# Folding w3 into w_out and setting attention phases between FFN half units

## The chip, the cores and the metric

One core of one Trainium2 chip. The metric is device time in microseconds (us) of the slowest core, here the only one, as the median of several executions.

## The reference

```python
# q, k, v: (8, 8, 576, 64) float32, heads 0-3 "local", heads 4-7 "strided"
scores = q @ k.T / 8
rel = pos[:, None] - pos[None, :]
mask_local   = (rel >= 0) & (rel < 32)
mask_strided = (rel >= 0) & (pos[None, :] % 32 == pos[:, None] % 32)
attn = softmax(where(mask, scores, -1e9)) @ v
x = attn as (4608 tokens, 512)
h = ((x @ w1) * (x @ w2)) @ w3        # w1, w2: 512x1024, w3: 1024x1024
out = h @ w_out                       # w_out: 1024x512
```

There is nothing between `@ w3` and `@ w_out`, so the two can be one matrix of 1024x512.

## The kernel before

Attention is computed for one pair of heads at a time. Local heads use tiles of 96 queries against 128 keys. Strided heads are first sorted by residue class, 7 classes of 18 tokens to a tile of 126. The FFN works on 384 tokens at a time (12 chunks). Five of its first halves are issued among the attention; the rest runs afterwards. All cuts are marked with `...`.

```python
def emit_ffn_ab(tch, pool):                      # first half: (x w1) * (x w2)
    for jc in range(8):
        for ci in range(4): nc.tensor.matmul(aps, w1h[:, ci, js], xT[ci][:, tok], ...)
        nc.scalar.copy(out=asb, in_=aps)
        for ci in range(4): nc.tensor.matmul(bps, w2h[:, ci, js], xT[ci][:, tok], ...)
        nc.vector.tensor_mul(abt[:, jc, :], bps, asb)

def emit_ffn_rest(tch):                          # second half
    for jc in range(8):                          # h = ab @ w3
        for ci in range(8):
            nc.tensor.matmul(hps, w3h[:, ci, js], abt[:, ci, :], ...)            # L142
        nc.scalar.copy(out=hts[:, jc, :], in_=hps)
    for ts in range(3):                          # out = h @ w_out
        for ci in range(8):
            nc.tensor.matmul(ops, hts[:, ci, bass.ds(ts*P, P)], woh[:, ci, :], ...)
        ...

def emit_att(b):
    for hp in range(4):
        ...
        # strided pairs: evict the transposed q or k and sort it by class
        nc.scalar.copy(                                                          # L175
            out=_ap(tT, 0, [[pit, P], [4, 4], [1, 4], [18, 32]]),   # writes 36 bytes apart
            in_=tp0.rearrange("p c (j1 j0) -> p c j1 j0", j0=32))   # reads in order
        ...
        for hj in range(2):                      # one head after the other
            ...                                  # scores, exp, mask, values, normalise, transpose
        # strided pairs: back into token order
        nc.vector.tensor_copy(                                                   # L264
            out=_ap(xT[cc], S * b, [[NTOK, P], [1, 32], [32, NB]]),
            in_=_ap(xPc, 0, [[S, P], [NB, 32], [1, NB]]))

for b in range(8):
    if b == 1: emit_weights()
    emit_att(b)
    if 2 <= b < 7: emit_ffn_ab(b - 2, psAB_)
for c in range(12):                              # after all attention
    if c not in abts: emit_ffn_ab(c, _pf)
    emit_ffn_rest(c)
```

The softmax here doesn't subtract the row's maximum and nothing guards it: scores larger than these inputs give would overflow.

## Time and profile before

| | before |
|---|---|
| time, median | 579.07 us (573.91 to 583.76) |
| profiled span | 574.6 us |
| TensorE busy, mean granted clock | 499.6 us, 0.906 |
| attention stage, 0 to 302 us | TensorE busy 233.8 us, clock 0.84 |
| FFN stage, 302 to 575 us | TensorE busy 265.9 us, clock 0.98 |

The page of the kernel before: the busy times of the engines, then the TensorE, clock and DMA rows of the 40 slices (each digit is tenths of a slice of 14.4 us), then the chain of waits by line.

```profile
PE 499.6 (87%) x3201; PEld 301.2 (52%) x3201; DVE 189.4 (33%) x657; ACT 289.2 (50%) x477; POOL 150.5 (26%) x243
...
PE   4868845888888898987868999999999999999997
...
PEclk9999955599999899886555999999999999999999
DMA  7998695658868687576620111111101010101001
...
PE hps L142 22%; PE ops L148 10%; PE aps L126 10%; ACT tT L175 9%; PE bps L131 9%; PE sps L231 5%; PE tps L249 4%; PE xps L241 4%; ACT pte L232 2%; DMA vts<-in_v_dram 1%; DVE xqs L244 1%; ACT w3h L115 1%; DVE xT_113 L264 1%; ACT asb L129 1%; DVE ptm L238 1%
```

The clock numbers need one caution: where a page has no record of the granted clock yet, it counts full speed. The record begins at 53.8 us in this trace. Before that, 96-column transposes (L249) start 80 ns apart, as they do in stretches recorded at clock 0.5 (80 ns at 262 to 313 us), and not 43 ns as at clock 1. So TensorE ran at half clock there too.

The busy share of 87% is an average over two stages with different limits. A table by stage shows it; the columns are the stretch, its length, busy time of TensorE, its weight loads, VectorE, ScalarE and GpSimd, then the clock, the DMA share and GB/s.

```profile
0.00:302.00 302.00, 233.79 (x1677) 151.03 (x1677) 153.87 (x590) 194.87 (x287) 150.16 (x243) 0.84 0.73 117
302.00:575.00 273.00, 265.85 (x1527) 150.15 (x1525) 35.50 (x68) 94.33 (x190) 0.33 (x1) 0.98 0.10 36
```

The second stage is one stream of matmuls. Here is a piece of its timeline (start, duration, what, how many):

```profile
403.73 5.53 PE L142 MATMUL hps<-abt,w3h 128*128 128x384 f16 x33
409.10 5.34 PE L148 MATMUL ops<-woh,hts 128*128 128x512 f16 x24
```

A run of matmuls lasts (number - 1) starts plus the duration of the last, 0.38 us for 512 columns; so (5.34 - 0.38) / 23 = 215.7 ns from start to start. The same sum for 384 columns gives 162.4 ns.

In the first stage the engines wait for each other. One copy stands out, the sorting eviction at L175:

```profile
L175 ACT CAST tT<-tp_1289 x1: 2352/2352/2352, 118.5 to 118.5; 128x512 f16<-128x512 f32 x1
...
L264 DVE COPY xT_113<-xPc x8: 1408/1422/1428, 39.9 to 299.5; 128x576 f16<-128x576 f16 x8
...
L253 ACT COPY xT_111<-tps x16: 632/632/633, 17.4 to 279.6; 64x576 f16<-64x576 f16 x16
```

That is 2352 / 512 = 4.6 ns an element on ScalarE; the plain copy of 576 elements at L253 takes 0.632 us, 1.1 ns an element. In the view of who waited for whom, this copy has the longest line of TensorE (total us, times, longest):

```profile
PE sps L231 <- ACT tT L175: 21.5, 14, 2.4
```

### The profile page before, as it was taken

Reading aid. Unit: us, or ns where it says so; the run is one execution under the profiler, and the core shown is the slowest. Engines: PE = TensorE matmul, PEld = TensorE weight load, DVE = VectorE, ACT = ScalarE, POOL = GpSimd, SP = SyncE. Lnnn points to the kernel's source line nnn. Section 1 sums busy time; section 2 is a strip of 40 time slices with the busy share of each in tenths; the row PEclk is TensorE's granted clock in tenths of the full one; section 3 lists DMA queues with packets and bytes.
Section 4 is the critical chain, followed back from the end, with each engine's and each line's share of the span. In section 5 each row is a group of like instructions: output and inputs, shape, how many; then the busy total and the mean of one; then the engine's idle time right before and its main releaser. Section 6 shows DMA issues by size and latency. Waiting matters only on the chain.

```text
span 574.6 us, 8898 instructions
## 1 busy us (share of the span) xinstructions
PE 499.6 (87%) x3201; PEld 301.2 (52%) x3201; DVE 189.4 (33%) x657; ACT 289.2 (50%) x477; POOL 150.5 (26%) x243
## 2 busy tenths in 40 slices
PE   4868845888888898987868999999999999999997
PEld 2544423555555455555644555555565655555563
DVE  1454414547566575745543000003021111203030
ACT  2874777385766758484561333333333333333332
POOL 5652224355655538255450000000000000000000
PEclk9999955599999899886555999999999999999999
DMA  7998695658868687576620111111101010101001
GB/s 159 189 210 204 169 226 89 87 82 101 109 88 103 80 117 95 81 88 87 80 13 4 56 55 46 47 38 38 53 3 56 0 56 1 55 15 42 37 19 55
DMA packets 160443, 45.00 MB, mean 78 GB/s; under 512 B 152720, under 2 KB 152720, under 8 KB 160400
## 3 DMA queue, kind: packets, MB, share of 16 engines
q1 hardware_dynamic: 86160, 38.82, 24.8%
q0 software_dynamic: 74240, 5.63, 17.8%
q8 instruction: 25, 0.41, 0.3%
q14 instruction: 18, 0.15, 0.1%
HBM read 40.37 MB, written 9.44 MB: 87 GB/s over the span
## 4 chain that ended last, share of the span: by engine, by line
PE 72%; ACT 15%; DVE 5%; issue 3%; DMA 3%; SPq 1%; POOL 0%; DVEq 0%; ACTq 0%; POOLq 0%
PE hps L142 22%; PE ops L148 10%; PE aps L126 10%; ACT tT L175 9%; PE bps L131 9%; PE sps L231 5%; PE tps L249 4%; PE xps L241 4%; ACT pte L232 2%; DMA vts<-in_v_dram 1%; DVE xqs L244 1%; ACT w3h L115 1%; DVE xT_113 L264 1%; ACT asb L129 1%; DVE ptm L238 1%
## 5 line engine op out<-in xcount | busy, mean ns | idle before, releaser
L133 DVE TENSOR_TENSOR abt<-bps,asb 128x384 f16<-128x384 f32 x96 | 53.2, 555 | 233.9 <-PE bps L131 210.5
L142 PE MATMUL hps<-abt,w3h 128*128 128x384 f16 x768 | 129.4, 330 | 0.7 <-DVE xPc L260 0.7
L212 POOL DMA_DIRECT2D vts<-in_v_dram x160 | 99.8, 652 | 74.2 <-PE xps L241 34.6
L142 PEld LDWEIGHTS <-w3h 128*128 128x128 f16 x768 | 75.9, 99 | 52.7 <-issue 2.9
L144 ACT CAST hts<-hps 128x384 f16<-128x384 f32 x96 | 45.9, 478 | 91.1 <-PE hps L142 91.1
L129 ACT COPY asb<-aps 128x384 f32<-128x384 f32 x96 | 49.2, 514 | 44.4 <-DVE abt L133 37.8
L232 ACT ACTIVATE pte<-sps 128x288 f16<-128x288 f32 (+2 forms) x128 | 51.8, 440 | 30.0 <-PE sps L231 19.7
L231 PE MATMUL sps<-tT 64*128 64x96 f16 (+1 forms) x352 | 43.3, 248 | 25.6 <-ACT tT L175 21.5
L148 PE MATMUL ops<-woh,hts 128*128 128x512 f16 x288 | 64.1, 379 | 0.0
L131 PEld LDWEIGHTS <-w2h 128*128 128x128 f16 x384 | 36.9, 100 | 28.5 <-issue 6.7
L231 PEld LDWEIGHTS <-tT 64*128 64x128 f16 (+1 forms) x352 | 27.3, 134 | 45.4 <-ACT tT L175 28.0
L126 PEld LDWEIGHTS <-w1h 128*128 128x128 f16 x384 | 36.2, 101 | 26.5 <-issue 4.5
L241 PE MATMUL xps<-vts,ptm 128*96 128x65 f16 (+1 forms) x352 | 44.0, 243 | 2.4 <-DVE ptm L238 1.1
L249 PE MATMUL tps<-id128h,xqs 96*64 96x96 f16 (+1 forms) x352 | 35.7, 248 | 11.2 <-DVE xqs L244 10.5
L148 PEld LDWEIGHTS <-hts 128*128 128x128 f16 x288 | 28.2, 98 | 32.7
L151 ACT COPY osb<-ops 128x512 f32<-128x512 f32 x36 | 21.1, 585 | 44.5 <-PE ops L148 41.7
L241 PEld LDWEIGHTS <-ptm 128*96 128x96 f16 (+1 forms) x352 | 35.5, 160 | 13.8 <-DVE ptm L238 4.8
L249 PEld LDWEIGHTS <-xqs 96*64 96x64 f16 (+1 forms) x352 | 24.5, 130 | 30.5 <-DVE xqs L244 19.5
L126 PE MATMUL aps<-xT_111,w1h 128*128 128x384 f16 x96 | 32.7, 340 | 5.7 <-ACT asb L129 5.7
L204 POOL DMA_DIRECT2D vts<-in_v_dram x32 | 18.8, 586 | 65.9 <-PE xps L241 28.4
L126 PE MATMUL aps<-xT_113,w1h 128*128 128x384 f16 x96 | 32.7, 341 | 2.7 <-DVE xT_113 L264 2.7
L244 DVE TENSOR_TENSOR xqs<-xps,rcp 96x384 f16<-96x384 f32 (+1 forms) x64 | 34.1, 533 | 0.5
(430 smaller groups left out, 619.9 us busy)
## 6 DMA issues: line engine op xcount, KB each, us to landing
out_dram<-osb SPq DMA_DIRECT2D x36, 256.0 KB, 2.0
stg<-in_q_dram SPq DMA_DIRECT2D x64, 128.0 KB, 2.5
stg<-in_k_dram SPq DMA_DIRECT2D x64, 128.0 KB, 2.8
st<-in_moe_w_dram SPq DMA_DIRECT2D x4, 2048.0 KB, 7.7
vts<-in_v_dram POOLq DMA_DIRECT2D x32, 80.0 KB, 3.5
vts<-in_v_dram POOLq DMA_DIRECT2D x128, 15.8 KB, 2.6
st<-in_moe_w_out_dram SPq DMA_DIRECT2D x1, 2048.0 KB, 8.4
stg<-in_q_dram SPq DMA_DIRECT2D x64, 16.0 KB, 2.6
```

The costliest lines, as they stand in the source:

```text
L126: nc.tensor.matmul(aps, w1h[:, ci, js], xT[ci][:, tok], start=(ci == 0), stop=(ci == DM // P - 1))
L129: nc.scalar.copy(out=asb, in_=aps)
L131: nc.tensor.matmul(bps, w2h[:, ci, js], xT[ci][:, tok], start=(ci == 0), stop=(ci == DM // P - 1))
L133: nc.vector.tensor_mul(abt[:, jc, :], bps, asb)
L142: nc.tensor.matmul(hps, w3h[:, ci, js], abt[:, ci, :], start=(ci == 0), stop=(ci == DF // P - 1))
L148: nc.tensor.matmul(ops, hts[:, ci, bass.ds(ts * P, P)], woh[:, ci, :], start=(ci == 0), stop=(ci == DF // P - 1))
L175: nc.scalar.copy(out=_ap(tT, 0, [[pit, P], [4, 4], [1, 4], [18, 32]]), in_=tp0.rearrange("p c (j1 j0) -> p c j1 j0", j0=32))
L212: nc.gpsimd.dma_start(vts[0:18 * na, t, 0:D], _ap(v[b, h], 7 * t * D, [[D, na], [32 * D, NB], [1, D]]))
L231: nc.tensor.matmul(sps[0:krows, i, :], lhs, rhs, start=True, stop=True)
L232: nc.scalar.activation(out=pte[0:krows, 0:nt, :], in_=sps[0:krows, 0:nt, :], func=AF.Exp, bias=0.0, scale=scale)
L241: nc.tensor.matmul(xps[0:qt, t, :], ptm[0:krows, i, :], vts[0:krows, t, :], start=True, stop=True)
L249: nc.tensor.transpose(tps[bass.ds(crow, 64), t, 0:qt], xqs[0:qt, t, :], id128h[0:qt, 0:qt])
```

## The change

The intent has three parts. (1) w3 @ w_out is computed once on the chip, so that the h product disappears from every chunk. (2) Attention is cut so that strided tiles hold whole classes (72 tokens, 4 classes of 18) and the two heads of a pair share instructions; re-ordering copies now walk the output in order and put the stride on the PSUM read; q, k, v come in large pieces through the SP queue and GpSimd casts them. (3) Attention becomes a list of 7 short TensorE steps per pair (score group 0, transpose of the next q, score group 1, transpose of the previous output, value group 0, transpose of the next k, value group 1). The steps of batch t + 1 are placed one by one between the 24 half units of FFN tile t (512 tokens; four matmuls of 512 columns each), and each TensorE instruction is kept in program order. Below, a fold is the making of one of the eight row blocks of w3 @ w_out; the opening is the time before the first FFN tile; steps or tiles are bare when nothing is placed between them; an eviction is the copy of a TensorE result out of PSUM, where TensorE writes, into SBUF.

```diff
-    NT = 384
+    NT = 512
+    LQ, LT = 96, 6
+    SQ, ST = 72, 8
+    def pe(ins):
+        return tc.keep_in_program_order(ins)
 ...
+    def ph_T(s, which):                       # transpose of q or k, both heads of a pair
+        for c in range(n):
+            pe(nc.tensor.transpose(ps[:, c * w:(c + 1) * w], ...))
+        if s.local:
+            o, i = t[:, 0:S].rearrange("x (p c) -> x p c", c=n), ps[:, 0:S].rearrange("x (c p) -> x p c", p=w)
+        else:
+            o, i = t[:, 0:S], ps[:, 0:S]
+        if which == "q":
+            nc.scalar.copy(out=o, in_=i)
+        else:
+            nc.vector.tensor_copy(out=o, in_=i)
 ...
+    def ph_S(s, g):                           # scores, the two heads by turns
+        for i in range(m):
+            for h in range(2):
+                pe(nc.tensor.matmul(sps[:, h, i * w:(i + 1) * w], s.tT["k"][r, ks:ks + P], ...))
 ...
+    def ph_PV(s, g):                          # values; 128 weight columns, the tail is zeros
+                pe(nc.tensor.matmul(xps[:, h, i * 65:(i + 1) * 65], ptm[0:kr, c0:c0 + P], ...))
 ...
-        for jc in range(DF // P):
-            hps = psF[0].tile([P, NT], FP32, tag="hps")
-            for ci in range(DF // P):
-                nc.tensor.matmul(hps, w3h[:, ci, js], abt[:, ci, :], ...)
-            nc.scalar.copy(out=hts[:, jc, :], in_=hps)
+    def fold_halves(jc):                      # once: 8 transposes and 8 matmuls of 512 columns
+        def tr(): ...                         # w3 rows -> w3T, evicted by VectorE and ScalarE
+        def done(ps): nc.vector.tensor_copy(out=w34[:, jc, :], in_=ps)
+        return [tr] + acc_halves(lambda kc: w3T[kc // 4][:, kc % 4, js], lambda kc: woh[:, kc, :], done)
 ...
+    def host(units, upto):
+        n = len(units); p0 = pos[0]
+        for i, u in enumerate(units):
+            u()
+            tgt = p0 + ((upto - p0) * (i + 1)) // n
+            while pos[0] < tgt:
+                stream[pos[0]](); pos[0] += 1
 ...
+    load_wo(); load_w3(0); load_w3(1)         # the opening
+    for jc in range(4): ...                   # four folds, alone
+    load_local(0); load_w3(2); load_w3(3); load_strided(0); load_w12()
+    host(later, 14)                           # four folds between 14 attention steps
+    load_local(1)
+    att_only(batch_end[0])                    # the other steps of batch 0, bare
+    load_strided(1)
+    for tch in range(NTILE):                  # tiles 0 to 6 host batches 1 to 7; 7 and 8 are bare
+        units = ab_halves(tch) + o_halves(tch)
+        ...
```

## The prediction

> What bounds it now. The page's span is 574.6 us. A table by stage splits it at 302 us. After that only FFN runs: TensorE is busy 266 of 273 us at clock 0.98, so this stage is bound by matmul columns (24 matmuls of 512 columns ran in 5.34 us: 215.7 ns start to start). Before it, attention: TensorE 234 of 302 us at mean clock 0.84 (0.59 in 250-300 us). The chain of waits there is led by ScalarE's scattered q/k eviction (L175, 2.35 us each, 64 of them; 150 us of ScalarE), then small matmuls.
>
> What the change removes and adds, in TensorE columns:
> - Fold: the h product (768 matmuls x 384 columns) becomes a one-time 64 x 512 plus 64 transposes. 768 x 162.4 ns = 125 us goes, about 17 us comes. FFN then needs 864 matmuls of 512 columns = 186 us, all on the critical path.
> - Attention: a pair takes 42 (local) or 56 (strided) matmuls instead of 46 or 40, all small. In a warm stretch six transposes of 96 columns take 0.44 us (42 ns apart), 65-column ones 46 ns, 126-column ones 55 ns. I estimate 50 ns x 1568 = 78 us for all 32 pairs, about 10 us per batch.
> - Scattered writes disappear (the L175 evictions, the 1.42 us L264 copies): class-complete chunks make eviction writes contiguous and put the stride on the PSUM read. The Trainium skill ("SBUF — State Buffer", cachelines) says strides past a line pay, for both memories; this trace shows it for writes (4.6 ns per element at L175 against 1.1 at L253), and no line shows a strided PSUM read. I assume about 0.7 us for 576 elements.
> - V no longer goes through the GpSimd queue in small packets. GpSimd instead casts about 10,750 elements per partition per batch: estimated 11-20 us a batch.
>
> Per stage:
> 1. Start: about 12 us until w_out and the first w3 rows are in and cast, 16 us for four serial folds, about 20 us for four folds mixed with attention, about 20 us of latency-bound attention steps: about 68 us. Weight loads are not the limit (a 2 MB piece landed in 7.7 us).
> 2. Seven tiles, each hosting one batch: 96 x 216 ns = 20.7 us of FFN + 10 us of attention + 2-4 us of bubbles (the single transpose bank, a matmul behind GpSimd's zero fills, the tile's start behind the last xT eviction) = about 33.5, together 235 us. VectorE needs about 21 us and ScalarE about 15 us of each by this trace's durations, so TensorE bounds it; clock near 1.0.
> 3. Two bare tiles, 42 us, and a tail of 3.
>
> Sum about 348; I say 350 us, range 325 to 382. Faster by over 2%: 0.99; within 2%: 0.005; slower: 0.005.
>
> What would show it. Right: TensorE clock above 0.95 from about 70 us to the end; a steady 31-35 us per tile; no eviction of 576 elements above 1 us; the chain of waits over 75% TensorE. Wrong: strided PSUM evictions at 2 us or more (then ScalarE/VectorE head the chain, +40 us or more); GpSimd copies near 2 ns per element with TensorE waiting on zero fills; a clock of 0.5 in the opening lasting past 80 us.
>
> What would make it wrong. High side: the fixed TensorE order turns each late eviction into an idle TensorE; in-order VectorE queues hold weight casts ahead of attention; GpSimd and VectorE slow each other (the skill's "GPSIMD Engine Reference", key points, says they share SBUF interfaces; this trace has no such overlap). Low side: the 64-row score matmuls of two heads overlap in the array, and the opening loads run ahead.

## More of the kernel before

The times of one kernel in one set of rounds lie within 2% of each other, mostly within 1%.

## The result, and the profile after

| | before | after |
|---|---|---|
| time, median | 579.07 us (573.91 to 583.76) | 313.54 us (312.88 to 314.86) |
| profiled span | 574.6 us | 311.9 us |
| TensorE busy, mean clock | 499.6 us, 0.906 | 277.8 us, 0.965 |

The ratio is 0.543 (95% interval 0.539 to 0.547). Ratios here are the mean time of one kernel's runs over the mean of the other's in the same rounds, so not quite the ratio of the medians quoted. The direction and most of the size were foreseen, but 313.5 us lies under the stated range of 325 to 382.

The page of the changed kernel; a slice is now 7.8 us:

```profile
PE 277.8 (89%) x2561; PEld 144.2 (46%) x2561; DVE 188.9 (61%) x361; ACT 134.6 (43%) x221; POOL 100.3 (32%) x192
...
PE   0285757689999999999999999999999999999994
...
PEclk9999897569999999999999999999999999999999
DMA  6999999998769989999895868660002001102003
...
PE ops L317 26%; PE bps L303 20%; PE aps L294 20%; PE ps L201 5%; PE sps L224 5%; PE xps L250 4%; DMA st<-in_moe_w_dram 3%; PE ps L266 3%; ACT pte L229 2%; DVE w_115 L350 1%; ACT xT_112 L273 1%; DVE w3T_117 L346 1%; DVE xqs L258 1%; PE ps L344 1%; DVE t L212 1%
```

The clock record begins at 16.9 us here; the first fold's matmuls of 512 columns, before that, start 0.43 us apart, twice 0.216. Counted at 0.5, the mean clock would be about 0.94 instead of 0.965 (my estimate).

By stage (opening; seven tiles that host a batch each; two bare tiles and the tail), and then one hosted tile:

```profile
0.00:65.20 65.20, 36.80 (x351) 21.74 (x352) 33.43 (x63) 24.27 (x36) 21.34 (x48) 0.86 0.99 268
65.20:266.00 200.80, 199.23 (x2023) 103.71 (x2020) 141.17 (x279) 97.92 (x165) 78.98 (x144) 0.99 0.64 151
266.00:312.00 46.00, 41.77 (x196) 18.71 (x194) 14.27 (x21) 12.38 (x21) 0.00 (x0) 0.98 0.14 52
...
124.50:153.20 28.70, 28.44 (x293) 14.84 (x292) 19.64 (x40) 14.26 (x25) 13.20 (x23) 1.00 0.92 212
```

TensorE is busy 199.2 of 200.8 us in the middle. The view of its waits there (66 to 300 us) has one line:

```profile
PE aps L294 <- ACT xT_112 L273: 1.5, 6, 0.3
```

A tile repeats every 28.7 us. Inside it, steps and half units follow each other like this:

```profile
108.95 0.30 PE L224 MATMUL sps<-t 64*128 64x72 f16 x8
109.19 0.43 PE L266 MATMUL ps<-id_79,xqs 96*128 96x96 f16 x6
109.45 0.38 PE L294 MATMUL aps<-xT_109,w1h 128*128 128x512 f16 x1
...
110.32 0.41 PE L250 MATMUL xps<-v16S_103,ptm 72*128 72x65 f16 x8
110.56 0.38 PE L303 MATMUL bps<-xT_109,w2h 128*128 128x512 f16 x1
```

From the start of one line to the start of the next is what a step costs: 0.24 us for eight score matmuls, 0.26 for six transposes, 0.24 for eight value matmuls. On ScalarE, the re-ordering evictions that now read with a stride are no slower than plain ones (L210 is half the one and half the other). On VectorE they are: the 16 of L212 that read with a stride took 0.71 to 0.76 us, its 16 plain ones 0.40 to 0.46. Two lines of ScalarE, then VectorE's:

```profile
L273 ACT COPY xT_111<-ps x8: 632/632/640, 61.1 to 262.7; 128x576 f16<-128x576 f16 x8
...
L210 ACT COPY t<-ps x32: 626/640/646, 30.4 to 253.7; 128x576 f16<-128x576 f16 x32
...
L212 DVE COPY t<-ps x32: 397/584/758, 32.3 to 258.2; 128x576 f16<-128x576 f16 x32
```

### The profile page after: what moved, and what is told of

Read it like the earlier page. It is cut to its first block, busy times and chain, and to the rows that moved or that the text cites. A ratio compares the mean times of both kernels' runs of the same rounds, so it can differ in the third digit from the quotient of the medians.

```text
span 311.9 us, 6533 instructions
## 1 busy us (share of the span) xinstructions
PE 277.8 (89%) x2561; PEld 144.2 (46%) x2561; DVE 188.9 (61%) x361; ACT 134.6 (43%) x221; POOL 100.3 (32%) x192
## 4 chain that ended last, share of the span: by engine, by line
PE 83%; DVE 6%; ACT 5%; DMA 3%; issue 1%; SPq 0%; DVEq 0%; ACTq 0%
PE ops L317 26%; PE bps L303 20%; PE aps L294 20%; PE ps L201 5%; PE sps L224 5%; PE xps L250 4%; DMA st<-in_moe_w_dram 3%; PE ps L266 3%; ACT pte L229 2%; DVE w_115 L350 1%; ACT xT_112 L273 1%; DVE w3T_117 L346 1%; DVE xqs L258 1%; PE ps L344 1%; DVE t L212 1%
## 5 line engine op out<-in xcount | busy, mean ns | idle before, releaser
L297 ACT COPY asb<-aps 128x512 f32<-128x512 f32 x72 | 42.2, 586 | 68.8 <-PE aps L294 51.3
L229 ACT ACTIVATE pte<-sps 128x576 f16<-128x576 f32 (+1 forms) x64 | 41.6, 650 | 36.7 <-PE sps L224 36.1
L173 POOL CAST t<-st 72x1024 f16<-72x1024 f32 x32 | 33.0, 1059 | 25.0 <-DMA st<-in_q_dram 15.1
L154 POOL CAST t<-st 96x768 f16<-96x768 f32 x32 | 26.9, 867 | 29.2 <-DMA st<-in_q_dram 17.1
L201 PEld LDWEIGHTS <-t 72*128 72x128 f16 (+1 forms) x448 | 25.1, 101 | 17.0 <-issue 4.0
L201 PE MATMUL ps<-id_79,t 72*128 72x72 f16 (+1 forms) x448 | 28.5, 206 | 3.1 <-ACT w3T_118 L347 2.8
L250 PEld LDWEIGHTS <-ptm 72*128 72x128 f16 (+1 forms) x448 | 23.2, 101 | 17.2 <-issue 2.2
L236 DVE TENSOR_TENSOR ptm<-pte,maskS 72x576 f16<-72x576 f16 x32 | 19.3, 603 | 17.7 <-ACT pte L229 17.5
L294 PE MATMUL aps<-xT_112,w1h 128*128 128x512 f16 x72 | 27.5, 382 | 1.6 <-ACT xT_112 L273 1.5
L294 PE MATMUL aps<-xT_109,w1h 128*128 128x512 f16 x72 | 27.8, 386 | 0.0
L303 PE MATMUL bps<-xT_109,w2h 128*128 128x512 f16 x72 | 27.6, 384 | 0.0
L294 PE MATMUL aps<-xT_111,w1h 128*128 128x512 f16 x72 | 27.5, 382 | 0.0
L294 PE MATMUL aps<-xT_110,w1h 128*128 128x512 f16 x72 | 27.5, 382 | 0.0
L303 PE MATMUL bps<-xT_110,w2h 128*128 128x512 f16 x72 | 27.3, 379 | 0.0
L303 PE MATMUL bps<-xT_112,w2h 128*128 128x512 f16 x72 | 27.3, 379 | 0.0
L303 PE MATMUL bps<-xT_111,w2h 128*128 128x512 f16 x72 | 27.2, 378 | 0.0
```

The lines of the kernel that those rows point to most:

```text
L154: nc.gpsimd.tensor_copy(out=t[:, hp], in_=stv[:, 2 * hp:2 * hp + 2].rearrange("p h c d -> p c h d"))
L173: nc.gpsimd.tensor_copy(out=t[:, hp], in_=stv[:, 2 * hp:2 * hp + 2].rearrange("p h c d -> p c h d"))
L201: pe(nc.tensor.transpose(ps[:, c * w:(c + 1) * w], src[:, c].rearrange("p h d -> p (h d)"), id16[0:w, 0:w]))
L229: nc.scalar.activation(out=pte[0:kr], in_=sps[0:kr, :, 0:288], func=AF.Exp, bias=0.0, scale=scale)
L236: nc.vector.tensor_mul(ptm[0:kr, 0:576].rearrange("p (a x) -> p a x", x=w), pte[0:kr].rearrange("p h (a x) -> p (h a) x", x=w), _ap(maskS, ...
L250: pe(nc.tensor.matmul(xps[:, h, i * 65:(i + 1) * 65], ptm[0:kr, c0:c0 + P], vt[0:kr, 2 * (s.hp % 2) + h, g * m + i, :], start=True, stop=T ...
```

## The experiments

My theory after the result: the whole middle is matmul columns back to back; the h product's columns are simply gone; hosting takes away the waits; and my price for attention in a tile was too high, both per matmul and in waits. The rival readings are that one part (the pinned order, the overlap of two heads, the walk of the evictions) did nearly all of it. Five runs also ask what bounds the opening. Not tested alone are the loads in large pieces with GpSimd's casts, and that two heads share instructions; what these are worth is not shown.

### The fold, done alone in the kernel before

```diff
-        for jc in range(8):  ...  matmul(hps, w3h, abt) ; copy(hts, hps)
-                nc.tensor.matmul(ops, hts[:, ci, ...], woh[:, ci, :], ...)
+                nc.tensor.matmul(ops, abt[:, ci, ...], w34[:, ci, :], ...)
+        emit_fold()            # at the start of the FFN stage
```

> Kernel before, with w3 and w_out folded at the start of its FFN stage and the h product gone; attention untouched. Theory (the FFN stage is bound by matmul columns): 768 x 162.4 ns = 124.7 us goes, 64 x 215.7 ns + 64 transposes + waits = 17 to 22 us comes, so about 103 to 108 us less than before: 472 to 478 us; the attention stage stays at about 302 us. Rival (without the h product the evictions on ScalarE and VectorE bind the stage): less than 80 us saved, TensorE busy under 90% after 320 us.

Measured: 470.89 us against 577.01 in the same rounds (ratio 0.8135, interval 0.807 to 0.820), 106 us less. That is what the theory of matmul columns gave (103 to 108 us less), though 1 us under the range named for the total. TensorE is busy 145.1 of the 150 us from 320 us on, so the rival falls.

### The fold, taken out of the changed kernel

```diff
-        units = ab_halves(tch) + o_halves(tch)
+        units = ab_halves(tch) + h_halves(tch) + o_halves(tch)   # 16 half units more, evicted by ScalarE
-    (all fold_halves; w34)
+    (w3 and w_out kept as they are; fewer buffers for abt to make room)
```

> Changed kernel with the h product put back (64 more matmuls of 512 columns per tile, evicted by ScalarE), no fold, the attention steps spread over 40 half units per tile instead of 24. Theory (every tile is TensorE columns back to back): +9 x 64 x 215.7 ns = +124 us, less 5 to 17 us that the opening loses of folds, so 420 to 432 us; a tile grows from 28.7 to 42.5 us. Rival (the order of work and not the fold makes the gain): under 380 us.

Measured: 436.41 us (ratio 0.7529), 123 us more than the changed kernel, 4 us above the range I had named. The reason is instructive: the opening got only 1.5 us shorter (its first FFN matmul starts at 63.96 us instead of 65.44). So 124.2 - 1.5 = 122.7 us is the columns' full price, and the folds, about 17 us of TensorE work, cost almost nothing where they stand. (In three runs with the same order of opening, after_again, narrow_pv and scores_by_head, it started at 66.09, 64.12 and 64.87 us, so 1.5 us is not clear of scatter.) TensorE waits there for loads and casts instead: in this run's opening 36.1 us of its waiting ends with GpSimd's casts of q and k.

### TensorE instructions not kept in order

```diff
-        return tc.keep_in_program_order(ins)
+        return ins
```

> Changed kernel, TensorE instructions no longer kept in program order: the scheduler may move them. Theory (the fixed interleaving is what leaves no gap in the tiles): gaps come back, tiles grow from 28.7 us to 30 us or more, total 320 to 360 us. Rival (pinning is worth nothing, dependencies alone give the same order in effect): within 1% of the changed kernel, 311 to 317 us.

Measured: 312.92 us (ratio 0.5407, interval 0.537 to 0.545). The theory falls, the rival holds: pinning is worth nothing here. The scheduler moved some instructions (the first FFN matmul came at 49.62 us), but in the tiles it kept a stream almost without waits. Its tiles repeat every 28.31 us, 0.4 less than 28.71, but tile 0, begun early, took so long that both kernels reach tile 1 together (at 95.92 and 95.01 us). The placing of steps in the program does the work, not the pin.

### Attention steps not spread

```diff
             u()
-            tgt = ...
-            while pos[0] < tgt: ...
+        att_only(upto)         # after the units
```

> Changed kernel, same instructions, but each tile runs its 24 FFN half units first and then the attention steps of the next batch with nothing between. Theory (hosting hides the latency of the eviction chain): the unhosted opening ran 17 steps in 15.5 us, 0.91 us a step against 0.24 hosted, so 197 steps x 0.67 us = about +130 us: 410 to 460 us, with a lower clock in those stretches. Rival (the steps are cheap by themselves, pairs already overlap each other): under 350 us.

What ran is a little milder than that text says: a tile calls the placing twice, so it has two blocks of 12 units and 14 steps each. Measured: 402.42 us (ratio 0.6958), 89 us more, so hosting matters but under the 98 to 148 us that I had expected. Its middle by stage:

```profile
65.30:356.00 290.70, 245.68 (x2034) 130.99 (x2032) 149.34 (x279) 98.31 (x168) 79.37 (x144) 0.83 0.42 106
```

The 90 us have two halves. TensorE is idle 290.7 - 245.7 = 45 us instead of 1.6. And it is busy 245.7 us instead of 199.2 for the same instructions, because the granted clock is 0.83 instead of 0.99. The record shows the granted clock at 1 for 13.7 us and then at 0.5 for 6.8, over and over. No single wait in that stretch is longer than 1.43 us; the first line of its TensorE waits:

```profile
PE sps L224 <- DVE xqs L258: 23.1, 28, 1.4
```

### Attention steps in groups of four

```diff
+            if i + 1 < n:
+                tgt = p0 + 4 * ((tgt - p0) // 4)
```

> Changed kernel, attention steps set between FFN half units four at a time (S0 Tq S1 T2, then PV0 Tk PV1 S0) instead of one at a time; the same instructions. Unhosted (all 28 at once) costs +88 us or 12.6 us a tile. Theory (no bubbles because two half units, 1.7 us, lie between a step and the step that needs its eviction): T2 now follows Tq after 0.24 us and waits about 1.3 us for the bank, S0 follows PV0 after 0.5 us and waits about 1 us, so 2 us a pair, 6 to 10 us a tile: +40 to +70 us. Rival (any FFN work nearby is enough): under +10 us.

Measured: 354.26 us (ratio 0.6139), 41 us more, just inside what the theory gave for the total; the rival falls. The tiles repeat every 33.8 us, 5.1 more than in the changed kernel, a little under the 6 to 10 named. Its TensorE waits, over the whole run:

```profile
PE sps L224 <- DVE xqs L258: 19.7, 15, 2.7
PE ps L266 <- ACT t L210: 10.8, 18, 0.8
...
PE sps L224 <- DVE t L212: 9.6, 17, 1.1
```

The first two are the ones named beforehand: the scores that need a PSUM buffer back from the normalising product, and the transpose that needs the one transpose bank back from ScalarE. In the third, scores wait for the evicted k. The clock stayed at 1.00 (94 to 270 us), so here the loss is waiting alone. This shows why the bubbles that I had budgeted were missing: spread singly, a step has about two half units, 1.7 us, before its eviction is needed, and an eviction with its latency fits in.

### Walking the re-ordering copies the other way

```diff
-  o, i = t[:, 0:S].rearrange("x (p c) -> x p c", c=n), ps[:, 0:S].rearrange("x (c p) -> x p c", p=w)
+  o, i = t[:, 0:S].rearrange("x (p c) -> x c p", c=n), ps[:, 0:S].rearrange("x (c p) -> x c p", p=w)
   (and the same for the output of strided pairs)
```

> Changed kernel, the three re-ordering evictions (q and k of local pairs, the output of strided pairs) walk their elements the other way round: PSUM read straight, SBUF written with a stride of 12 or 16 bytes. Same values. Theory (the stride costs on the write and not on the read, and the fixed order then leaves TensorE idle): ScalarE's 32 such copies take 2.0 to 2.7 us instead of 0.64, VectorE's 16 take 1.2 to 1.5 instead of 0.6, and as the single transpose bank comes free only about 2.4 us later by schedule, tiles grow by 2 to 6 us: +15 to +45 us. Rival 1 (the slack between steps swallows it): copies as slow, but under +5 us. Rival 2 (the read side costs the same as the write side, or nothing does): the copies stay near 0.64 us.

Measured: 382.08 us (ratio 0.6626), 69 us more, over the top of my expectation. The lines of the three copies:

```profile
L210 ACT COPY t<-ps x32: 624/1357/2091, 30.9 to 319.2; 128x576 f16<-128x576 f16 x32
...
L212 DVE COPY t<-ps x32: 396/1232/2092, 33.5 to 323.7; 128x576 f16<-128x576 f16 x32
...
L273 ACT COPY xT<-ps x16: 2702/2710/2732, 69.2 to 331.7; 128x576 f16<-128x576 f16 x16
```

Minimum, median and maximum are in ns; half of the first two groups are plain copies and stayed fast. The turned ones went to 2.09 us on both engines (from 0.64 us on ScalarE and 0.75 on VectorE) and to 2.71 us. VectorE's was the surprise (I had said 1.2 to 1.5). The slack of 1.7 us no longer suffices; TensorE waits for these copies (below, 66 to 340 us), and the clock falls to 0.92 (95 to 203 us). Rival 1 and rival 2 both fall.

```profile
PE aps L294 <- ACT xT L273: 16.5, 8, 2.2
PE ps L266 <- ACT t L210: 16.4, 14, 1.8
```

### The same lesson in the kernel before

```diff
-    out=_ap(tT, 0, [[pit, P], [4, 4], [1, 4], [18, 32]]), in_=tp0.rearrange("p c (j1 j0) -> p c j1 j0", j0=32)
+    out=_ap(tT, 0, [[pit, P], [18, 32], [1, 16]]),        in_=_ap(tp0, 0, [[..., P], [1, 32], [32, 16]])
     (and L264 likewise)
```

> Kernel before, only the walk of two copies turned round: ScalarE's q/k eviction and VectorE's last re-ordering copy now write contiguous runs and read with a stride. Theory (the write side costs): 2.36 us falls to 0.55 to 0.7 us and 1.42 us to 0.3 to 0.8 us, 64 x 1.75 = 112 us less of ScalarE, of which the chain of waits (about 9% of the span in that copy) lets 35 to 80 us through: 500 to 545 us. Rival (four-dimensional walks cost, whichever side is strided): copies within 20% of what they were, and time within 2%.

Measured: 538.7 us (ratio 0.9339, interval 0.930 to 0.938), 38 us less for two turned walks with the same values. The copies:

```profile
L175 ACT CAST tT<-tp x32: 580/585/593, 22.0 to 260.0; 128x512 f16<-128x512 f32 x32
...
L264 DVE COPY xT<-xPc x16: 640/674/684, 36.4 to 269.0; 128x576 f16<-128x576 f16 x16
```

The walk at L264 has as many dimensions as before, so there the side of the stride alone made the difference, and the rival falls. This also shows a slip of mine, in the prediction and in the expectation: the copies are 32, not 64, so they cost 75 us of ScalarE and not 150. ScalarE's busy time fell from 289.2 to 236.5 us. The time landed in my range although the sum behind it was twice too large, which was luck.

### Value matmuls with narrow weights

```diff
-  matmul(xps[:, h, ...],    ptm[0:kr, c0:c0 + P], ...)
+  matmul(xps[0:w, h, ...],  ptm[0:kr, c0:c0 + w], ...)
```

> Changed kernel, value matmuls with 96 or 72 weight columns instead of 128 (the padding read no more). In the kernel before, such matmuls with 96 weight columns started 46 ns apart, and in the changed kernel with 128 weight columns 31 ns apart. Theory (my 50 ns per small matmul was too dear because it came from narrow weights; full weights load faster): the value steps grow from 0.18 and 0.24 us to about 0.28 and 0.33, 64 x 0.1 = +5 to +7 us in all. Rival (the width of the weights costs nothing, 65 streamed columns decide): under +1 us.

Measured: 316.83 us (ratio 0.5489, against 0.5426 for spread_fold, below, a run of the same rounds that is as fast as the changed kernel): about 3.5 us more. In the trace, local value steps went from 0.18 to 0.25 us (six matmuls, from 30 to about 45 ns apart), strided ones only from 0.24 to 0.28. The difference is real, and as the steps add up (32 x 0.07 + 32 x 0.035 = 3.4 us), but half of what I had expected: it explains 0.4 us of a tile, not the 3.3 that I was off in attention.

### Scores head by head

```diff
-        for i in range(m):
-            for h in range(2):
+        for h in range(2):
+            for i in range(m):
```

> Changed kernel, score matmuls of one head after those of the other, instead of alternating between the upper and lower 64 rows of the array. Now six start about 18 ns apart, but the step still takes 0.23 us to the next step's start. Theory (overlap of the two heads is nearly eaten up by a pause behind it): 6 x 41 or 8 x 33 ns = 0.25 us a step, +1 to +3 us in all. Rival (the overlap of two heads is what made attention cheap, as my low side had it): +8 us or more.

Measured: 315.01 us (ratio 0.5461), 1.5 us above the changed kernel, inside the theory and hardly above noise; by the traces, tiles repeat every 28.78 us instead of 28.71. A step takes 0.24 to 0.25 us instead of 0.23 to 0.24. But the edit did not do what the expectation took for granted: head by head, the matmuls still start close together (on average 17 and 21 ns apart, against 15 and 20 by turns), so this run shows no step without overlap. Another comparison settles it: in the changed kernel eight 72-column transposes take 0.259 us to the next start and eight 72-column score matmuls 0.236, and six of 96 columns 0.257 and 0.234. So overlap can be worth about 0.02 us a step, 0.2 us a tile; it is not what made attention cheap.

### The opening: five runs and a base

```diff
 spread_fold:   host(folds 4 and 5, 14 steps); host(folds 6 and 7, all other steps)
 local1_early:  load_w12 first half; load_local(1); load_w12 second half
 att_first:     load q, k, v of batch 0 first; 8 steps bare; folds 0-3 among the others; folds 4-7 in tile 0
 att_first2:    the same with 22 steps bare
 fold_late:     w1, w2 before w_out, w3; all steps of batch 0 bare; all folds in tile 0
```

> Changed kernel, the last four folds spread over all 31 opening attention steps instead of the first 14. The run without any fold had an opening of 64 us against 65, so folds seem to cost nothing there. Theory (the opening is bound by loads and the casts behind them): no change, within 2 us of the changed kernel. Rival (the 17 steps left bare are bound by latency, which FFN-like work would hide): opening 6 to 12 us shorter.

Measured: 312.32 us (ratio 0.5426): no change, first FFN matmul at 65.36 us. The bare steps were not what held it.

> The changed kernel once more, as the base for the runs on the same chip. Expected 311 to 315 us.

Measured: 315.16 us (ratio 0.5467, interval 0.545 to 0.549). The next two runs were made in the same rounds on the same chip.

> Changed kernel, only the order of loads in the opening changed: the first loads of batch 1 (which the opening's last steps need) go between the halves of w1 and w2 instead of behind them. The load queues were 99% busy over the opening's 65 us. Theory (the opening is bound by what is loaded before its last step): about 2 MB of w1 and w2 move behind the gate, at 268 GB/s about 7 us; 2 to 7 us faster than the changed kernel. Rival (the opening is bound by the latency of bare steps and folds, not by loads): within 1.5 us.

Measured: 312.09 us (ratio 0.5418, interval 0.540 to 0.544), 3 us or 0.9% faster than the changed kernel in the same rounds, with the first FFN matmul at 62.81 us against 66.09. The theory's low end, and the only version that is faster than the changed kernel clear of noise, by little.

> Changed kernel with a new opening: q, k, v of batch 0 are loaded first, its attention starts at once, four folds are hosted among its later steps, and the last four folds (with their w3 rows) are hosted in the first tile. Theory (the opening is bound by loads): tile 0 starts at about 45 to 50 us instead of 65, grows by 9 us of folds, and the total falls by 6 to 12 us to 301 to 307 us. Rival (bound by the latency of the steps, which a cold TensorE makes worse): tile 0 starts after 58 us and the total is not lower than 311 us.

Measured: 322.88 us (ratio 0.5599), 8 us slower. Tile 0 started earlier (60.43 us), but TensorE had stood 12.7 us at the first fold, whose w3 rows now came behind q, k and v:

```profile
31.00 1.04 PE L344 MATMUL ps<-id,t 128*128 128x128 f16 x8 [12.71 <-DVE t L130]
```

and the folds placed in tile 0 lengthened it. My theory, as I had turned it into an opening, lost.

> As att_first, but 22 opening steps run before the first fold, so that TensorE does not stand at a fold whose w3 rows are not there; four folds hosted on the last 11 opening steps, four in the first tile with their transposes one fold ahead. Theory (loads bound the opening, 17.5 MB by 65 us, and work can run under them): tile 0 starts at 46 to 52 us, total 303 to 309 us. Rival (latency of bare steps): tile 0 after 58 us, total 314 us or more.

Measured: 325.53 us (ratio 0.563), tile 0 at 62.15 us. TensorE stood 4.6 us at the fold and then 7.6 us for the casts of batch 1.

> Loads in the order q, k, v of batch 0, w1, w2 (batch 1 in between), then w_out and w3; opening attention bare, all eight folds in the first tile between its two halves. Theory (load-bound): tile 0 starts at 40 to 48 us, and the total is 302 to 309 us, as the 17 us of folds now lie under loads that still run until 65 us. Rival (latency of bare steps on a cold clock): tile 0 after 52 us and 314 us or more.

Measured: 336.55 us (ratio 0.5798). Tile 0 did start at 39.67 us, as I had expected, but then stood 9.4 us for batch 1's strided q and k, whose loads now came last, and the folds in the tile paused at each pass through the single transpose bank (1 to 1.8 us each); tile 1 started at 119.08 us, against 95.01 in the changed kernel. From tile 1 on, all these versions run 28.7 us a tile. An early start of tile 0 is worth nothing if the data that tile 0 must host comes later.

What bounds the opening stays partly open. Loads do in part (the earlier load gained 3 us; the queues are 99% busy), folds and bare steps by themselves do not, and three attempts to use the time better by another order failed.

## Why the prediction was wrong

Added by stage, prediction against profile: opening 68 against 65.2 us; seven hosted tiles 235 (33.5 each) against 200.8 (28.7 each); two bare tiles with the tail 45 against 46. **The step that failed is number 2, "20.7 us of FFN + 10 us of attention + 2-4 us of bubbles"**: 34 of the 36 us by which the sum missed are there. The mechanism was right (TensorE bounds the tile), two of its terms were mis-sized:

- *"I estimate 50 ns x 1568"*, 10 us a batch. Measured: the 28 steps of a batch (12 transposing steps of 0.26, 8 score steps of 0.235, 4 value steps of 0.18 and 4 of 0.24) make 6.7 us, which is 34 ns for each of 196 matmuls. I had averaged spacings of the old kernel's 96-, 65- and 126-column matmuls over a kernel whose matmuls have 65, 72 or 96. Against 50 ns each, the values made 1.1 us less, the scores 0.9, the 72-column transposes 0.8 and the 96-column ones 0.3. The section "Back-to-back issue gap" of the Trainium skill's page "TensorE: Matmul & The Clock Gate" has the form that would have served: columns / 2.4 + 2.5 ns, so 32.5, 42.5 and 29.6 ns for 72, 96 and 65 columns. (The section gives it for matmuls by themselves and has other figures for streams; those do not fit here, see the end.) The traces show medians of 32, 42 and 30 (transposes, transposes, values), and 215.7 against 215.8 for 512 columns. An estimate of 6.8 us a batch from it (24 x 42.5 + ... for each kind) would have been right. Neither the full-width weights (0.4 us a tile) nor the overlap of two heads (at most about 0.2) is the main cause.
- *"2-4 us of bubbles"*. Measured: 0.26 us of waiting a tile, and about 1 us at the joints between steps and units (28.7 - 20.7 - 6.7 = 1.3 in all). Most of that stands in one place: a score step starts 0.311 us after the last 512-column matmul before it, other steps 0.216 us after; 8 x 0.095 = 0.8 us. What makes this pause is not shown. I had seen the single transpose bank as a risk without setting the 1.7 us of FFN work between two uses of it against an eviction of 0.64 to 0.75 us. The run in groups of four brought 5.1 us a tile back, mostly at the waits I had named, so the spreading is the cause.

Point by point, the rest:

- The FFN stage as pure columns, 125 us out: right; 106 us net when done alone, 123 us when undone.
- About 17 us for the folds: near as work (with them TensorE is busy 36.8 us in the opening, without them 16.7, part of it at half clock), wrong as time. Taking them out shortened the opening by 1.5 us. The opening's total of 68 was near, but as a sum of serial pieces it was right for a wrong reason: loads and casts run beside them.
- "Weight loads are not the limit": wrong for the opening. The DMA share was 0.99 over its 65.2 us, and moving one load forward gained 3 us; one piece's landing time of 7.7 us did not show how full the queues would be.
- "Scattered writes disappear", about 0.7 us for a strided PSUM read: right; 0.63 to 0.64 us on ScalarE, 0.71 to 0.76 on VectorE. The count of 64 copies and 150 us of ScalarE was wrong (32, 75 us).
- VectorE about 21 us and ScalarE about 15 us a tile: 19.6 and 14.3. GpSimd 11 to 20 us of casts a batch: 13.2 with its fills. TensorE never waited for it in the tiles.
- Clock over 0.95 from the opening on: 0.99. The chain of waits over 75% TensorE: 83%.
- Of the high-side risks, GpSimd and VectorE do slow each other: the mask product, which reads two SBUF tensors, has a median of 455 ns (459 for local pairs), but 15 of the 64 took over 500, up to 2344. Each of the 15 began under a GpSimd cast and ended 306 to 315 ns after the end of a cast, as if it had waited for it. The page "GPSIMD Engine Reference" (key points) says that they share SBUF interfaces; this trace agrees. In the tiles TensorE waited for none of them; in the opening once, 0.35 us.
- VectorE's weight casts did hold up attention in the opening: at 58.66 us TensorE had waited 2.08 us for a normalising product that stood behind a cast of 1.73 us.
- Of the low side, "score matmuls of two heads overlap" is true and nearly worthless.

Undone one at a time from the changed kernel, the h product is worth 123 us, the spreading 89 and the walk of the copies 69. They add to more than the 266 us gained; that waits and clock count in more than one of them would explain it, but no run separates this.

## What to carry to other kernels

Price small matmuls by their own column count, not by an average from other widths, and before budgeting bubbles compare, for each buffer, the work between two uses with the eviction that frees it. When a copy must re-order, walk it so that SBUF is written in order and put the stride on the read; turning two such walks round was worth 38 us in the old kernel, and turning three back cost 69 in the new. Spread short dependent steps singly between long independent ones: bunched four at a time they cost their waits (41 us), and fourteen at a time their waits and then, through the granted clock, as much again (89 us).

## What the Trainium skill lacked or had wrong

- "TensorE: Matmul & The Clock Gate", § Back-to-back issue gap, gives a sustained spacing of about 131 ns for 512 columns and 81 ns for 128 in real kernels. Here streams of weight load and matmul run at 215.7 ns for 512 columns and 32 to 42 ns for 72 to 96; the "isolated" form of the same section fits all of them.
- The same page, § Why this matters for your kernels, asks for no idle gaps over about 3 us to keep the clock. With the steps bunched no wait was over 1.43 us, and the mean clock of the tiles was still 0.83. (The page's § A second HAM failure mode: psum-queue depth-cycling, says that frequent short pauses can do this, but gives no length.)
- "SBUF — State Buffer" tells of 16-byte lines in SBUF and 8-byte lines in PSUM (there of matmuls) without separating reads from writes. Here a PSUM read 144 to 192 bytes apart cost ScalarE nothing (0.63 to 0.64 us for 576 elements) and VectorE 0.3 us (192 bytes apart 0.75 us, in order 0.45), while 2-byte SBUF writes 12 or 16 bytes apart took 2.09 and 2.71 us on ScalarE and 2.09 us on VectorE.
- "ScalarE: Activation LUTs" states one element per cycle for every function and does not mention the output's stride: 512 elements written 36 bytes apart took 2.35 us, in order 0.585 us.
